# Order tables for all five engines, halved dense groups and paired layer norms in a two-layer attention and token-mixing kernel

## The chip, the cores and the metric

The kernel runs on one core of one Trainium2 chip. Its time is device microseconds of one execution; the time before is 478.1 us, the median of 6 runs from 476.24 to 480.12. A profile is one more execution that the hardware profiler recorded. Its engines are PE (TensorE's matmuls, with PEld for the weight loads), DVE (VectorE), ACT (ScalarE), POOL (GpSimd) and SP (SyncE, which issues the DMAs).

## What is computed

Two layers, the same weights in both, on x of 2048 tokens by 512 features in bf16. Each layer adds sliding-window attention and then a token-mixing MLP to x:

```python
def _A_ref(x, wqkv, wo):
    H = 32; Dh = D // H; W = 256
    q, k, v = ...                        # x @ wqkv, 32 heads of 16
    scores = einsum("bhqd,bhkd->bhqk", q, k) * (Dh ** -0.5)
    mask = (idx[:, None] - idx[None, :] >= 0) & (idx[:, None] - idx[None, :] < W)
    p = softmax(where(mask, scores, -1e9))
    return einsum("bhqk,bhkd->bhqd", p, v) ... @ wo
def _B_ref(x, w1, b1, w2, b2):
    h = _layernorm(x)
    u = gelu(einsum("bsd,sf->bdf", h, w1) + b1)      # mixes tokens: 2048 -> 1792
    return einsum("bdf,fs->bds", u, w2) + b2         # 1792 -> 2048, back to (s, d)
x = x + _A_ref(_layernorm(x)); x = x + _B_ref(_layernorm(x))     # twice
```

`_B_ref` is given a layer norm of x and takes another, so the kernel applies one formula for both (`twice` in `ln_block`).

## The kernel before

**Tiles and stages.** The 2048 tokens are 16 tiles of 128 partitions, grouped in four chunks of 512 tokens. For a chunk m the stages are:

- `prepare` (L1052): in layer 1 first the previous MLP's second product for its four tiles (`y_block`, L1032, 14 matmuls of 512 columns in entries of four, four, four and two); then the layer norm of the tiles (`ln_block`, L682: two statistics instructions on DVE, L686 and L688, two small ones on POOL, L691 and L693, and the scaling on DVE, L697), and `qkv` (L727).
- `qkv`: four transposes on PE into PSUM (L747), their copies to `xhT` (L731 on DVE or L733 on ACT), then K and Q of head group o (`proj`, four matmuls of 512 columns, L764) and V for four pairs of 64-token blocks (`vproj`, L794, in two entries of eight matmuls each). K is written as `kbd`, two masked copies. For chunk 0 of both layers ACT makes them straight from PSUM (L773, the set `KACT`), else a staging copy and two POOL instructions do (L780).
- `attention` (L826): for each of four head groups, four (chunk 0) or five pieces. A piece is one score entry on PE (L848, 8 or 12 matmuls into two pairs of PSUM banks), two exps on ACT of 1024 elements each (L860, some of 768), and masks on DVE (L873, L876). The pieces of a head group end in one P·V entry on PE (L894, 72 or 112 matmuls). Its result is copied by DVE (L938), its denominators travel over SP's queue: `rr` (L940), reciprocal on DVE (L947), `rscr` to DRAM (L949), `md` back, broadcast (L952), with four `cs` moves beside them (L944); POOL multiplies (L956). The last head group of the last chunk takes its denominators from matmuls instead (L907).
- `wo_block` (L962): the output projection (L966), added to x on DVE (L970), and the layer norm for the MLP.
- `u_part` (L998): the first product of the MLP for some chunks, 14 output tiles (L1012). Partial sums are held in `ub` (L1021, L1024); the last part ends in Gelu on ACT (L1027).

`STEPS` (L125) gives the order in which a layer's stages are recorded. In layer 0 parts u0, u1, u2 and U3 are separate, in layer 1 u0 and u1 are one.

**Scores are counted below** from 0 in layer 0 (0 to 75) and on in layer 1 (76 to 151).

**What sets the order.** Nothing is issued as it is recorded. `op` (L171) notes an operation with the engines that may run it, what it reads and writes, and a cost. `schedule` (L350) then runs a list scheduler: at each step `_pick` (L264) offers each engine's best candidate, scores first, P·V next, dense work by a priority that `fprio` (L708) makes from the place of recording plus a table of offsets, `RANK` (L21). `_place` (L215) gives PSUM banks and buffers, with a limit on the banks of each class (`small`, `big`, `sc`). `reorder` (L420) then moves entries by the offsets of a second table, `MOVES` (L35), and `emit` (L429) writes each engine's list with the semaphore waits it needs. `mm_group` (L714) cuts a dense product in entries of `STEP` = 4 matmuls, which is the grain at which other work can come between.

All loads go through SP, in the order of its list. At the start these are x tiles 0 to 3 one by one, then V's columns of wqkv (512 KB), x tiles 4 to 7 (512 KB), K's first block, x tiles 8 to 11, Q's first block (128 KB each), a bias, K's other blocks (384 KB), a bias, Q's other blocks, and later x tiles 12 to 15 and Wo. w1 comes in 28 loads of 256 KB a layer through four buffers (L981), w2 in 56 of 128 KB (L992).

## Time and profile before

| | |
|---|---|
| median of 6 runs | 478.1 us |
| profiled execution, its own time | 479.17 us |
| its span | 477.4 us |
| PE, DVE, ACT, POOL busy | 438.0, 365.9, 327.1, 126.7 us |
| exps (L860) | 304, 284.1 us busy |
| first exp starts, last exp of layer 0 ends | 16.45 us, about 174 us |
| L1012 and L1035, matmuls of 512 columns | 448 each, 108.3 and 103.7 us busy |
| chain that ended last | PE 64%, ACT 21%, DVE 7% |

A busy time is the union of an engine's instructions. PE's matmuls overlap in their pipeline, so the 380 ns of one are not its pace: forty-two matmuls of 512 columns in a row take 9.06 us, 0.216 each. "Idle before" with a releaser names what ended the wait.

### The profile page before, as it was taken

Reading aid. Unit: us, or ns where it says so; the run is one execution under the profiler, and the core shown is the slowest. Engines: PE = TensorE matmul, PEld = TensorE weight load, DVE = VectorE, ACT = ScalarE, POOL = GpSimd, SP = SyncE. Lnnn points to the kernel's source line nnn. Section 1 sums busy time; section 2 is a strip of 40 time slices with the busy share of each in tenths; the row PEclk is TensorE's granted clock in tenths of the full one; section 3 lists DMA queues with packets and bytes.
Section 4 is the critical chain, followed back from the end, with each engine's and each line's share of the span. In section 5 each row is a group of like instructions: output and inputs, shape, how many; then the busy total and the mean of one; then the engine's idle time right before and its main releaser. Section 6 shows DMA issues by size and latency. Waiting matters only on the chain.

```text
span 477.4 us, 15704 instructions
## 1 busy us (share of the span) xinstructions
PE 438.0 (92%) x6830; PEld 208.1 (44%) x6830; DVE 365.9 (77%) x746; ACT 327.1 (69%) x372; POOL 126.7 (27%) x197
## 2 busy tenths in 40 slices
PE   7889867889989789999989999999999999999997
PEld 4355433353333344455444453444543444444443
DVE  6998988879989979764687888989976786952222
ACT  1999998798989970545998799789888872061000
POOL 3222453271531213010012623352373131200000
PEclk9999999899999999999999999999999999999999
DMA  8513231222253424232054224251325545524654
GB/s 248 150 40 92 68 97 51 75 74 76 63 151 91 135 85 119 81 89 66 5 141 118 73 74 121 71 133 31 83 57 149 138 119 140 145 76 137 180 168 133
DMA packets 83993, 49.47 MB, mean 104 GB/s; under 512 B 14676, under 2 KB 78164, under 8 KB 83924
## 3 DMA queue, kind: packets, MB, share of 16 engines
q1 hardware_dynamic: 83924, 48.46, 36.5%
q8 instruction: 54, 0.88, 0.8%
q14 instruction: 15, 0.12, 0.1%
HBM read 41.43 MB, written 2.59 MB: 92 GB/s over the span
## 4 chain that ended last, share of the span: by engine, by line
PE 64%; ACT 21%; DVE 7%; DMA 2%; SPq 2%; issue 2%; POOL 1%; POOLq 0%
ACT pt L860 19%; PE PS L1012 18%; PE PS L1035 17%; PE PS L894 7%; PE PS L764 6%; PE PS L848 6%; PE PS L966 4%; PE PS L794 4%; DVE pt L876 1%; DMA w1b<-in_B_w_dram 1%; DVE cs L938 1%; PE PS L613 1%; ACT kbd L773 1%; SPq L992 1%; SPq L944 1%
## 5 line engine op out<-in xcount | busy, mean ns | idle before, releaser
L860 ACT ACTIVATE pt<-PS 128x1024 bf16<-128x1024 f32 (+1 forms) x304 | 284.1, 1027 | 33.1 <-PE PS L848 30.8
L1012 PE MATMUL PS<-xh_sb,w1b 128*128 128x512 bf16 x448 | 108.3, 384 | 2.4 <-DMA w1b<-in_B_w_dram 1.0
L1035 PE MATMUL PS<-ub,w2b 128*128 128x512 bf16 x448 | 103.7, 380 | 0.0
L848 PE MATMUL PS<-qT,kbd 32*128 32x64 bf16 (+4 forms) x1632 | 60.7, 244 | 20.3 <-ACT pt L860 11.0
L1012 PEld LDWEIGHTS PS<-xh_sb,w1b 128*128 128x128 bf16 x448 | 40.2, 98 | 56.3 <-issue 7.3
L956 POOL TENSOR_TENSOR oT<-cs,md 128x512 bf16<-128x512 f32 x30 | 39.3, 1309 | 93.3 <-DMA cs<-cs 51.2
L764 PE MATMUL PS<-xhT,wqkv 128*128 128x512 bf16 x256 | 62.5, 381 | 1.4 <-DVE vt L731 0.9
L1035 PEld LDWEIGHTS PS<-ub,w2b 128*128 128x128 bf16 x448 | 41.3, 98 | 50.1 <-issue 3.9
L1024 DVE TENSOR_TENSOR ub<-PS,ub 128x512 f32<-128x512 f32 x70 | 46.0, 684 | 17.6 <-PE PS L1012 17.3
L876 DVE TENSOR_TENSOR pt<-pt,ldm 128x1024 bf16<-128x1024 bf16 (+1 forms) x80 | 54.8, 699 | 3.2 <-ACT pt L860 3.1
L848 PEld LDWEIGHTS PS<-qT,kbd 32*128 32x128 bf16 x1632 | 23.3, 92 | 76.3 <-ACT pt L860 43.6
L780 POOL TENSOR_SCALAR kbd<-stg,par 128x512 bf16<-128x512 bf16 x48 | 38.1, 803 | 65.4 <-DVE stg L731 55.9
L938 DVE COPY cs<-PS 128x512 f32<-128x512 f32 x60 | 39.1, 684 | 16.3 <-PE PS L894 15.5
L1040 DVE SCALAR_TENSOR_TENSOR x_sb<-PS,bcol,x_sb 128x512 bf16<-128x512 f32 x32 | 23.3, 745 | 35.7 <-PE PS L1035 35.5
L1027 ACT ACTIVATE ub<-ub,bcol 128x512 bf16<-128x512 f32 x28 | 18.5, 713 | 45.9 <-DVE ub L1024 45.8
L894 PE MATMUL PS<-pt,vt 64*18 64x64 bf16 (+4 forms) x3040 | 40.4, 247 | 5.5 <-ACT pt L860 2.7
L873 DVE TENSOR_TENSOR pt<-pt,ldm 128x512 bf16<-128x512 bf16 (+1 forms) x104 | 40.2, 409 | 4.3 <-ACT pt L860 4.2
L686 DVE BATCH_NORM_STATS2 stats<-x_sb 128x6 f32<-128x512 bf16 x64 | 43.1, 682 | 0.5
L691 POOL TENSOR_SCALAR rstd<-agg 128x2 f32<-128x2 f32 (+1 forms) x40 | 9.4, 235 | 121.4 <-DVE agg L688 120.3
L894 PEld LDWEIGHTS PS<-pt,vt 64*18 64x18 bf16 x3040 | 31.5, 85 | 15.7 <-ACT pt L860 5.5
L764 PEld LDWEIGHTS PS<-xhT,wqkv 128*128 128x128 bf16 x256 | 21.9, 98 | 30.5 <-issue 4.3
L794 PE MATMUL PS<-wqkv,xhT 128*64 128x256 bf16 x512 | 33.6, 275 | 1.6 <-issue 0.6
(54 smaller groups left out, 327.0 us busy)
## 6 DMA issues: line engine op xcount, KB each, us to landing
w2b<-in_B_w_dram SPq DMA_DIRECT2D x112, 128.0 KB, 2.4
w1b<-in_B_w_dram SPq DMA_DIRECT2D x56, 256.0 KB, 3.4
md<-rscr SPq DMA_DIRECT2D x30, 256.0 KB
cs<-cs SPq DMA_DIRECT2D x120, 32.0 KB, 2.5
out_dram<-x_sb SPq DMA_DIRECT2D x16, 128.0 KB, 1.8
x_sb<-in_A_x_dram SPq DMA_DIRECT2D x3, 512.0 KB
wqkv<-in_A_wqkv_dram SPq DMA_DIRECT2D x2, 384.0 KB, 5.3
x_sb<-in_A_x_dram SPq DMA_DIRECT2D x4, 128.0 KB
```

The source lines that it names most:

```text
L686: op("vector", lambda e, t=t: e.bn_stats(stats[:, t, :], x_sb[:, t, :]), reads=[f"x{t}"], writes=[f"st{t}"], cost=dve_cost(512))
L764: mm_group(ft, 4, lambda e, c: e.matmul(PS[:, ft.slot, :], lhsT=wqkv[:, c, which * 512 + o * P:which * 512 + (o + 1) * P], rhs=xhT[:, tx.s ...
L794: last = e.matmul(PS[64 * hf:64 * hf + 64, ft.slot, sc * 256:(sc + 1) * 256], lhsT=xhT[:, tx.slot, c, tok:tok + 64], rhs=wqkv[:, c, 1024:1 ...
L848: last = e.matmul(PS[:, bank(r), c0 * 64:(c0 + nb) * 64], lhsT=kbd[32 * r:32 * r + 32, tkk.slot, jj, :, :].rearrange("p h n -> p (h n)"), ...
L860: return e.activation(pt[:, tp.slot, 2 * u:2 * u + 2, 0:n], PS[:, b0:b0 + 2, 0:n], ACTF.Exp, scale=SMSCALE)
L873: return e.tensor_tensor(v, v, msk.unsqueeze(1).to_broadcast([P, 4, w]), op=ALU.mult)
L876: return e.tensor_tensor(v, v, msk.unsqueeze(1).unsqueeze(1).to_broadcast([P, 4, k, w]), op=ALU.mult)
L894: last = e.matmul(PS[32 * r:32 * r + 18, tO[h].slot, q0 * 64:(q0 + nb) * 64], lhsT=vt[64 * h:64 * h + 64, tvv.slot, jj, 4 * o + r, :], rhs ...
L938: op("vector", lambda e, tO=tO[h], tc=tc, h=h: e.tensor_copy(cs[:, tc.slot, h], PS[:, tO.slot, :]), reads=[tO[h]], writes=[(tc, h)], cost= ...
L1012: out_ = e.matmul(PS[:, tu.slot, :], lhsT=w1b[:, tw.slot, s, tt * P:(tt + 1) * P], rhs=xh_sb[:, 4 * m + s, :], start=(n == 0 and s == 0), ...
L1024: op("vector", lambda e, tu=tu, ft=ft: e.tensor_tensor(uacc(ft), PS[:, tu.slot, :], uacc(ft), op=ALU.add), reads=[tu] + uk(ft), writes=uk( ...
L1035: mm_group(ft, NFT, lambda e, fc: e.matmul(PS[:, ft.slot, :], lhsT=w2b[:, tws[fc // W2F].slot, fc % W2F, k * P:(k + 1) * P], rhs=uT(fc), s ...
```

## The change

- **Order.** `schedule`, `_pick`, `RANK` and the class limits in `_place` go. `follow` takes one written list of recorded operations for each engine, `ORDER`, and walks all five, to give buffers and banks in the order of the same cost estimates. It makes no choice of order or engine. `MOVES` is applied after it, with new values.
- **Halved groups.** `STEP` is 2 in layer 0 and 4 in layer 1, for projections, Wo and the U parts but the last.
- **Layer norm in pairs.** Chunk 0's tiles are normalised two at a time too, as those of the other chunks: one L691 and one L693 for two tiles.
- **Loads.** Recorded order of the first loads: x tiles 0 to 3, K's first block, Q's first block, V's columns, the rest. In the built program SP issues them as `ORDER` and `MOVES` say: x tiles 0 to 3, V's columns, x tiles 4 to 7, K's first block, Q's first block, x tiles 8 to 11, K's others, Wo, x tiles 12 to 15, Q's others.
- **K's copies** in chunk 0 may run on DVE as well, one after the other. In the built program all 16 are on ACT, as before. One other copy of layer 0 goes from ACT to DVE.
- Some operations get tags, with no effect on the program.

The diff, tables and repeated parts cut:

```diff
 NTR, DTR = (4, 4), 600
 EVACT = {(0, 0), (0, 1), (1, 0), (1, 1)}
 XHP = set()
-RANK = (
...
+ORDER = (
...
 )
 MOVES = (
...
 )
 KACT = {(l, 0, o) for o in range(4) for l in range(2)}
@@ -215,17 +348,12 @@
     def _place(self, o):
 
 
-        t, got, taken, wcls = 0.0, [], {}, {}
+        t, got, taken = 0.0, [], {}
         for tl in o.tiles:
             if tl.slots is not None:
                 continue
             pool = tl.pool
             used = taken.setdefault(id(pool), set())
-            q = pool.classes.get(tl.cls)
-            if q:
-                c = wcls[tl.cls] = wcls.get(tl.cls, 0) + tl.n
-                if q[0] + c > q[1]:
-                    return None
             when = {s: max([x.done for x in ops], default=0.0) for s, ops in pool.free.items() if s not in used}
             if tl.n == 2:
...
-    def _pick(self, e, cand, ready, free, mode):
...
-    HOLD = 600.0
-    WINDOW = ({0: 400.0, 1: 250.0, 2: 50.0}, {0: 150.0, 1: 400.0, 2: 400.0})
+
     layer = 0
-    SLACK = {"scalar": 60.0, "tensor": 0.0}
 
     HAM = 3413.3
-    WARM = (216.0, 0.45)
     warm = None
 
     def _dummy(self):
@@ -347,48 +419,53 @@
             t += d
         return t - t0
 
-    def schedule(self):
+    def follow(self, orders):
+
         self.dummies = []
         self.busy, self.rates, self.ported = {}, [0.5], [0.0, 0.0]
         free = {e: 0.0 for e in self.ENGS}
-        cand = {e: [] for e in self.ENGS}
-        ready = {}
+        ready = {o.idx: 0.0 for o in self.ops}
         self.order = {e: [] for e in self.ENGS}
-        dma_free = 0.0
-        mode = None
-        for o in self.ops:
-            if o.ndeps == 0:
-                ready[o.idx] = 0.0
-                for e in o.engs:
-                    cand[e].append(o)
-        left = len(self.ops)
+        ptr = {e: 0 for e in self.ENGS}
+        lists = {}
+        for e, order in zip(self.ENGS, orders):
+            lists[e] = []
+            for i in order:
+                if i < 0:
+                    o = self._dummy()
+                    self.dummies.append(o)
+                    ready[o.idx] = 0.0
+                else:
+                    o = self.ops[i]
+                o.eng = e
+                lists[e].append(o)
+        dma_free, mode = 0.0, None
+        left = sum(map(len, lists.values()))
         while left:
             best = None
             for e in self.ENGS:
-                if cand[e]:
-                    got = self._pick(e, cand[e], ready, free[e], mode)
-                    if got and (best is None or got[0] < best[0]):
-                        best = (got[0], e, got[1])
+                if ptr[e] == len(lists[e]):
+                    continue
+                o = lists[e][ptr[e]]
+                if o.ndeps:
+                    continue
+                t = free[e] + (SWITCH if e == "tensor" and o.mode != mode else 0.0)
+                t = max(ready[o.idx], t)
+                if o.port:
+                    t = max(t, self.ported[e == "vector"])
+                if any(tl.slots is None for tl in o.tiles):
+                    at = self._place(o)
+                    if at is None:
+                        continue
+                    t = max(t, at[0])
+                if best is None or t < best[0]:
+                    best = (t, e, o)
             if best is None:
...
+                raise RuntimeError("orders are stuck")
             m, e, o = best
...
-            for x in o.engs:
-                cand[x].remove(o)
-            o.eng = e
+            ptr[e] += 1
+            left -= 1
             o.fn, o.cost = o.engs[e]
-            if o.idx < 0:
-                self.dummies.append(o)
             self._alloc(o)
             o.start = m
             if o.dma:
...
@@ -627,11 +699,9 @@
         def load_w(a, b):
             op("sync", lambda e: e.dma_start(wqkv[:, :, a * P:b * P], w_src[:, :, a * P:b * P]),
                writes=[f"w{i}" for i in range(a, b)], dma=True, cost=(b - a) * 420, lat=2300.0, prio=-1e6)
-        load_x(0, 1)
-        load_x(1, 2)
+        for t in range(4):
+            load_x(t, t + 1)
         load_w(4, 5)
-        load_x(2, 3)
-        load_x(3, 4)
         load_w(0, 1)
         load_w(8, 12)
         load_w(5, 8)
@@ -701,7 +771,7 @@
                     engs["gpsimd"] = (f, 760)
                 op(engs, None, reads=[f"x{t}", f"ag{t}", f"rs{t}"], writes=[f"xh{t}"], port=True)
 
-        STEP = 4
+        STEP = (2, 4)
 
         groups = [0]
 
@@ -709,12 +779,13 @@
 
             k = groups[0]
             groups[0] += 1
-            return 1e6 + len(g.ops) + (RANK[k] if k < len(RANK) else 0) + 1e-4 * k
+            return 1e6 + len(g.ops) + 1e-4 * k
 
         def mm_group(dst, n, mk, reads, cols=512, prio=None, holds=(), tag=""):
             prio = fprio() if prio is None else prio
-            for k0 in range(0, n, STEP):
-                k1 = min(n, k0 + STEP)
+            st = STEP[g.layer]
+            for k0 in range(0, n, st):
+                k1 = min(n, k0 + st)
 
                 def f(e, k0=k0, k1=k1):
                     last = None
@@ -769,11 +840,16 @@
                     op(*evac(lambda: qT[:, tq[o].slot, :], lambda: PS[:, ft.slot, :]), reads=[ft], writes=[tq[o]], prio=-1e4)
                     return
                 if kact:
+                    kp = []
                     for h in range(2):
-                        op("scalar", lambda e, h=h: e.activation(
-                            kbd[:, tk[o].slot, :, h, :], PS[:, ft.slot, :].rearrange("p (s n) -> p s n", n=64), ACTF.Copy,
-                            scale=par[:, h:h + 1]), reads=[ft, ("par", h)], writes=[(tk[o], h)], cost=act_cost(512, 1),
-                           prio=-1e4)
+                        src = lambda: PS[:, ft.slot, :].rearrange("p (s n) -> p s n", n=64)
+                        kp.append(op({
+                            "scalar": (lambda e, h=h: e.activation(kbd[:, tk[o].slot, :, h, :], src(), ACTF.Copy,
+                                                                   scale=par[:, h:h + 1]), act_cost(512, 1)),
+                            "vector": (lambda e, h=h: e.tensor_scalar(kbd[:, tk[o].slot, :, h, :], src(), par[:, h:h + 1],
+                                                                      0.0, op0=ALU.mult, op1=ALU.add),
+                                       dve_cost(512, psum=True, ptrs=1))},
+                            None, reads=[ft, ("par", h)], writes=[(tk[o], h)], prio=-1e4, after=kp[:1]))
                     return
                 op(*evac(lambda: stg[:, ts.slot, :], lambda: PS[:, ft.slot, :]), reads=[ft], writes=[ts], prio=-1e4)
                 for h in range(2):
@@ -1000,1 +1076,1 @@
-            cls, st = ("big", 1) if last else ("small", STEP)
+            cls, st = ("big", 1) if last else ("small", STEP[g.layer])
...
@@ -1053,9 +1129,7 @@
                 for t in range(4 * m, 4 * m + 4):
                     if layer:
                         y_block(t, w2t, cls)
-                    if m == 0:
-                        ln_block([t], False)
-                    elif t % 2:
+                    if t % 2:
                         ln_block([t - 1, t], False)
                 Q[m], K[m], V[m] = qkv(m, cls)
             for step in STEPS[layer].split():
@@ -1077,7 +1151,7 @@
             op("sync", lambda e, t=t: e.dma_start(out_v[:, t, :], x_sb[:, t, :]), reads=[f"x{t}"], dma=True, cost=500, lat=1000.0,
                prio=1e5)
 
-        g.schedule()
+        g.follow(ORDER)
         g.reorder(MOVES)
         block = es.enter_context(nc.Block())
         g.emit(block)
```

## The prediction

> **What bounds the kernel now.** I read the page's busy times first, then busy time by stretch, then the order of time of ACT and PE around each long idle time of ACT.
>
> ```profile
> PE 438.0 (92%) x6830; PEld 208.1 (44%) x6830; DVE 365.9 (77%) x746; ACT 327.1 (69%) x372; POOL 126.7 (27%) x197
> PEclk9999999899999999999999999999999999999999
> ...
> 16.40:174.50 158.10, 134.77 (x2862) 64.39 (x2860) 140.52 (x291) 145.17 (x162) 55.53 (x76) 0.98 0.30 83
> 174.50:223.50 49.00, 48.97 (x373) 23.61 (x374) 33.76 (x64) 17.87 (x27) 7.28 (x17) 1.00 0.34 99
> 223.50:391.70 168.20, 159.24 (x3011) 75.46 (x3007) 138.85 (x287) 146.06 (x161) 54.97 (x74) 1.00 0.34 92
> 391.70:474.00 82.30, 81.19 (x476) 37.04 (x474) 39.29 (x69) 12.68 (x18) 4.30 (x9) 1.00 0.49 140
> 85.20:88.60 3.40, 3.25 (x50) 1.29 (x39) 2.94 (x6) 1.76 (x2) 0.27 (x1) 0.50 0.51 159
> ```
>
> The stretches give us, then busy PE, PEld, DVE, ACT, POOL, then granted clock. Layer 0's attention (16.4 to 174.5) has ACT busy 92% of the time and PE 85%: ACT sets its pace. The dense stretches (174.5 to 223.5, and from 391.7) are PE alone, 99 to 100%. Layer 1's attention has PE at 95%, ACT at 87%. So a microsecond taken from ACT's idle time in layer 0's attention reaches the end, since after its last score PE runs without idle time into layer 1; elsewhere only a shorter PE helps.
>
> ACT's idle time between first and last exp of layer 0 is 158.1 - 145.2 = 13 us. The lines that carry it:
>
> ```profile
> 57.97 1.94 ACT L860 ACTIVATE pt<-PS 128x1024 bf16<-128x1024 f32 x2 [0.59 <-PE PS L848]
> 75.84 1.94 ACT L860 ACTIVATE pt<-PS 128x1024 bf16<-128x1024 f32 x2 [2.13 <-PE PS L848]
> 89.72 1.94 ACT L860 ACTIVATE pt<-PS 128x1024 bf16<-128x1024 f32 x2 [2.76 <-PE PS L848]
> 128.23 3.98 ACT L860 ACTIVATE pt<-PS 128x1024 bf16<-128x1024 f32 x4 [0.51 <-PE PS L848]
> 139.08 1.02 ACT L860 ACTIVATE pt<-PS 128x1024 bf16<-128x1024 f32 x1 [1.02 <-PE PS L848]
> ...
> 135.36 1.04 PE L1012 MATMUL PS<-xh_sb,w1b 128*128 128x512 bf16 x4 [0.43 <-ACT pt L860]
> 136.33 1.40 PE L894 MATMUL PS<-pt,vt 64*18 64x128 bf16 x112
> 137.66 1.04 PE L1012 MATMUL PS<-xh_sb,w1b 128*128 128x512 bf16 x4
> 138.62 0.40 PE L848 MATMUL PS<-qT,kbd 32*128 32x128 bf16 x12
> ```
>
> ACT waits for a score (L848) each time, and the score stands behind a lump on PE: a dense group of four, the 112 P·V matmuls, another dense group. A pair of exps takes 1.9 us, such a lump 3.0.
>
> **What the Trainium skill says.** "ScalarE: Activation LUTs", What ACT_TABLE_LOAD costs: an ACTIVATE takes 186 ns + 0.833 ns per element, and neighbours overlap by 93 ns. For 1024 elements 1,039 ns, one every 946; the trace has 1,038 and five in 4.78 us, so it agrees and an exp cannot be made shorter by order. "TensorE: Matmul & The Clock Gate", What's actually happening: half or full clock, decided by activity in free-running windows of about 3.4 us. The trace agrees: 0.50 in 85.2 to 88.6 and in 105.7 to 109.1, each behind a stretch with PE busy at most 1.9 of 3.4 us. "DMA: Bandwidth & Descriptors", Queues, rings and completion order: transfers that SyncE issues share one row of rings, taken in ring order; so a weight load moved behind others starts later. No run here isolates that.
>
> **The change part by part.** I compared the order of the built instructions with the order before.
>
> *Loads.* The source lists K's and Q's first blocks ahead of V's, but the order table does not: the program issues x tiles 0 to 3, V's 512 KB, x tiles 4 to 7, K's first block, Q's first block. Only Q's first block moves, ahead of x tiles 8 to 11. K's was issued at 3.66 us and lands some 5.2 later, 8.9. On PE, however, K and Q of head group 0 now stand behind three of V's eight half-groups, not behind all.
>
> *Start.* The last transposed tile is copied by 10.6 (ACT 9.99 + 0.58, DVE 10.21 + 0.42). Then K: four matmuls, 0.97, to 11.5 (before 12.50 to 13.5). Two K copies on ACT 1.27, to 12.8. Q follows K on PE to 12.4; its DVE copy stands behind three statistics of 0.65, so 12.8 + 0.69 = 13.5; score 0.4, first exp near 14.0 instead of 16.45. But ACT's work up to the fifth score's exp is the same set (8 K copies, 8 exps, 3 other copies): before from 12.61 to 26.04, of it 0.38 idle, so 13.05 us. After: 11.5 + 13.05 + 1.2 waiting for Q = 25.75. Gain 0.3 to 0.5, and one copy fewer on ACT in the layer (7 instead of 8, 0.6): **-1.0**. DVE takes that copy, 0.68, beside 12% idle time.
>
> *Halved groups.* In layer 0 projections, Wo and all U parts but the last go from four matmuls an entry to two: 90 more entries, the same matmuls. The totals before each fourth score are within 0.9 us of before; what changes is which side of a score a half falls. Behind P·V lumps, idle ACT time: score 20 0.59 loses a half V group 0.47; score 28 2.13 loses half a Wo group, 0.43; score 34 2.76 loses two U matmuls, at half clock 0.43 each (the warm-up, at half clock, has 12 in 4.88), 0.86 in all; score 53 0.51 loses its whole U group in front, all 0.51; score 58 1.02 loses two halves, 0.86; score 70 loses its 0.23. Sum 3.36. The halves go elsewhere: scores 48 and 59 now have 1.73 of dense work ahead of them, and an interval of that size shows 0.23 idle (132.45 and 149.25): +0.46. **-2.9**.
>
> *Mode changes.* PE changes between matmul layouts 342 times, before 331; ten of the eleven stand before the ninth score. One costs 0.11: a lone group of four takes 0.97, eight in a row 1.83. That is 1.1 us where PE idles 3.4 of 20 to 40 us; at nothing, and +1.1 if that cover is gone.
>
> *LN in pairs.* Eight POOL instructions fewer (0.2 and 0.56 us), hidden, POOL being busy 27%. A tile waits for its partner: in layer 1's first chunk the transpose of tile 1 stands 3.3 us of PE work behind tile 0's last y matmul, and the chain between them took about 3.4 (213.55 to 216.79 and its hops). **+0.2**, bounds 0 and 0.5; behind it on PE stand three more transposes and V.
>
> *SyncE's order.* Q's other three blocks are now issued behind Wo and x tiles 12 to 15, 1.05 MB more; at the first slice's 248 GB/s that is 4.2 us, landing near 17.7 instead of 13.46. Their first reader on PE comes near 18, and ACT has exps until 21. Nothing; at worst +2. Late in layer 1, loads 15 and 16 of w1 stand behind md's last load, which waits for a round trip through DRAM:
>
> ```profile
> 395.42 0.65 SPq L952 DMA_DIRECT2D md<-rscr  x1
> ...
> 399.54 3.61 PE L1012 MATMUL PS<-xh_sb,w1b 128*128 128x512 bf16 x16 [1.04 <-DMA w1b<-in_B_w_dram]
> ```
>
> Load 16 was issued at 394.20 and 15 at 393.02; they would go out near 395.6 and 396.6, with one 256 KB load less ahead of 16. The same PE instruction waits for it; dense work follows with no cover. **+0.3**, bounds -0.5 and +2.
>
> *Other order.* Layer 1's attention keeps its intervals but for swaps of one place: 0, bounds -1 and +1.
>
> Sum: -1.0 - 2.9 + 0.2 + 0.3 = -3.4. The profiled execution took 479.17 (span 477.4 and 1.8 around it), 1.1 above the median of 478.1. From the median, **474.7**; from the profiled one, 475.8. A difference of 0.5%, 2.4 us, is about what a measurement of this kernel can tell from no change.
>
> **Rivals.** *The clock takes it back.* If the steadier order does not lift PE out of half clock and two more windows fall to it, each costs half of 3.4 us: +3.4, so 478. For it: idle PE time in 81.8 to 85.2 comes from intervals that don't change; against: mean clock 0.98 leaves only two such windows. The same mechanism the other way, both windows gone, gives 471.3.
>
> *Mode changes cost more than 0.11.* Eleven changes in the stage where ACT is starved of scores: a lone score takes 0.40, and idle times of 0.16 to 0.45 stand before several. At 0.31 each (3.4 / 11) they eat the gain, from 0.53 ((3.4 + 2.4) / 11) the kernel is slower than can be mistaken; at 0.6, 478.1 - 3.4 + 6.6 = 481.3. For it: PE is nearly full from 8 to 20 us; against: 3.4 us idle after that.
>
> *SyncE becomes late.* PE waits 2 us for w1's loads instead of 0.3 and 2 us for Q's blocks: 474.7 + 1.7 + 2 = 478.4. For it: the lines above, 5.2 us from issue to landing; against: w1's 28 loads at 256 KB take 3.4 in the median, and three dense groups stand ahead of the reader of load 15.
>
> **How the numbers follow.** Sum as worked out 0.58 (its own range 472.5 to 477), both slow windows gone 0.08, two more slow windows 0.16, dear mode changes 0.10, late SyncE 0.08. Below 475.7: four fifths of the first and all of the second, 0.54. Above 480.5: the dear mode changes and tails of two others, 0.17. The rest, 0.29, is within. The range, 470.8 to 481, leaves out the tails.
>
> **What would show it.** First exp near 14 us; ACT's idle time before scores 28, 34 and 58 down to about 1.7, 1.9 and 0.2, and its sum in layer 0's attention from 13 to 9 or 10; last exp of layer 0 some 3.5 us earlier, near 170; the two dense stretches as long as before. Wrong if PE's idle time in the first 40 us grows, if PE waits for wqkv near 18 us, if a wait on w1b over 2 us shows in layer 1's last U part, or if more than two windows show half clock.

## The result and the profile after

The changed kernel takes 481.8 us in the median of the executions taken with the prediction (474.97 to 485.67, 35 of them), the kernel before 478.8 beside it (72). Ratio 1.0014, 95% interval 0.9996 to 1.0032: no difference that the measurement can tell from none, where 474.7, 0.7% faster, was forecast, and the median lies just above the range of 470.8 to 481. A median here counts every execution, a ratio leaves out those more than 1.5% above the fastest of their kernel (15 of the changed kernel's 35 here, 11 of 22 in r5 below, at most three in any other), which is why the two can differ by some tenths of a per cent. By medians the changed kernel is 0.6% slower here, and 0.3 and 0.2% in r1 and r9 below.

The profiled execution took 478.96 us (span 477.2, before 477.4). First its page, the busy line and the clock, then busy time by stretch with the columns as before (us; PE, PEld, DVE, ACT, POOL; clock; DMA), the stretches set at the changed kernel's own ends of stages:

```profile
PE 436.4 (91%) x6830; PEld 206.6 (43%) x6830; DVE 369.1 (77%) x747; ACT 326.7 (68%) x371; POOL 123.8 (26%) x189
PEclk9999999899999999999999999999999999999999
```

```profile
13.66:173.50 159.84, 138.69 (x2900) 65.56 (x2899) 140.73 (x299) 146.56 (x164) 54.20 (x76) 0.99 0.32 87
173.50:221.70 48.20, 47.67 (x370) 23.18 (x370) 33.09 (x64) 18.02 (x27) 6.32 (x13) 1.00 0.33 95
221.70:390.80 169.10, 157.38 (x3004) 75.47 (x2999) 145.41 (x289) 146.18 (x160) 54.27 (x73) 1.00 0.34 90
390.80:474.60 83.80, 82.39 (x480) 37.07 (x478) 39.67 (x67) 12.70 (x18) 5.36 (x11) 1.00 0.50 143
86.70:90.10 3.40, 3.40 (x20) 0.91 (x18) 1.98 (x3) 1.94 (x2) 0.00 (x0) 0.50 0.28 67
```

Two things are to be seen. Layer 0's attention starts earlier (13.66 against 16.45) and ends earlier, and one stretch at half clock is left of two. But in layer 1's attention, third line, PE is busy 157.4 of 169.1 us, 93%, where it had been 159.2 of 168.2, 95%: PE, which sets that stage's pace, now stands idle 11.7 us instead of 9.0. And DVE is busy longer, 145.4 us against 138.9 there, with two instructions more (289 against 287).

ACT's order of time where the forecast had named its idle times (columns: start, busy time in us, engine and line, operation, count, and in brackets the idle time before it with its releaser; the bracketed waits at 73.24, 87.73, 90.67, 135.53 and 137.98 are those ahead of scores 28, 34, 35, 58 and 59):

```profile
73.24 3.77 ACT L936 ACTIVATE pt<-PS 128x1024 bf16<-128x1024 f32 x4 [0.51 <-PE PS L924]
...
87.73 1.94 ACT L936 ACTIVATE pt<-PS 128x1024 bf16<-128x1024 f32 x2 [3.38 <-PE PS L924]
90.67 2.85 ACT L936 ACTIVATE pt<-PS 128x1024 bf16<-128x1024 f32 x3 [1.00 <-PE PS L924]
...
135.53 1.94 ACT L936 ACTIVATE pt<-PS 128x1024 bf16<-128x1024 f32 x2 [0.61 <-PE PS L924]
137.98 1.94 ACT L936 ACTIVATE pt<-PS 128x1024 bf16<-128x1024 f32 x2 [0.51 <-PE PS L924]
```

Score 28's wait fell from 2.13 to 0.51, score 58's from 1.02 to 0.61, but score 34's grew from 2.76 to 3.38, ahead of and into the half-clock stretch, and score 35 behind it has a new one of 1.00. What of this is due to the order is taken up below.

Where the time went is told best by the start of each score's first exp, changed kernel minus kernel before, in us, from the two traces. The first row is this profile; the next two are two more profiles of the same kernel (r1 and r9 below). The last is r3 below, which has layer 0 in the order of the kernel before, layer 1 in that of the changed kernel, and ran at full clock in both layers' attention.

| profile | score 0 | 12 | 44 | 75 (last of layer 0) | 76 (layer 1) | 116 | 151 (last) |
|---|---|---|---|---|---|---|---|
| changed | -2.79 | -0.97 | -3.03 | -2.29 | -1.84 | -2.84 | -0.88 |
| changed, r1 | -3.00 | -1.18 | -3.68 | +0.04 | +0.09 | -0.58 | +3.06 |
| changed, r9 | -3.32 | -1.49 | -6.06 | -1.38 | -0.93 | -2.10 | +0.12 |
| r3 | -0.49 | -0.36 | -3.10 | -1.91 | -1.04 | -2.13 | -0.31 |

The profile of the kernel before had two stretches at half clock in layer 0, so it is a slow measure there: r3, with the same layer 0 order, is 1.9 us ahead of it at score 75. Against r3 the changed kernel is 0.4 us ahead at score 75 in its first profile, 2.0 behind in r1 (each with a stretch at half clock near 85 us), and in r9, at full clock, 3.0 ahead at score 44 and 0.5 behind at score 75. One profile against another is good to a microsecond or two at best, as the three of one kernel show. But the pattern is plain: what start and layer 0 gain is given back, late in layer 0 in r1 and r9, and in the second half of layer 1's attention (score 116 is near 310 us of 222 to 391) in all four rows, 1.8 to 3.6 us between score 116 and the last. The 3.6 are r1's, which had a second stretch at half clock there, from 354.0 to 357.4 us.

Here is one of the places in layer 1, from the order of time of the changed kernel, VectorE, GpSimd and TensorE around 348 us:

```profile
346.92 0.41 DVE L949 TENSOR_TENSOR pt<-pt,ldm 128x512 bf16<-128x512 bf16 x1
347.25 1.67 DVE L767 TENSOR_SCALAR xh_sb<-x_sb,agg,rstd 128x512 bf16<-128x512 bf16 x1
348.85 1.28 DVE L802 CAST stg<-PS 128x512 bf16<-128x512 f32 x2
...
346.31 1.24 POOL L763 TENSOR_TENSOR rstd<-rstd,mhalf 128x2 f32<-128x2 f32 x1
347.51 1.26 POOL L1032 TENSOR_TENSOR oT<-cs,md 128x512 bf16<-128x512 f32 x1
...
347.99 0.40 PE L924 MATMUL PS<-qT,kbd 32*128 32x64 bf16 x12
350.18 0.40 PE L924 MATMUL PS<-qT,kbd 32*128 32x128 bf16 x12 [1.79 <-DVE stg L802]
```

One xh_sb, which takes 0.41 us elsewhere, takes 1.67: it begins beside the rstd power on GpSimd and does not end before oT, which follows at once, has ended at 348.77. Behind it in VectorE's order stand the two copies into stg, and behind those PE waits 1.79 us with a score. In the kernel before the same two copies follow a mask, with no GpSimd instruction that holds them up:

```profile
348.74 0.41 DVE L873 TENSOR_TENSOR pt<-pt,ldm 128x512 bf16<-128x512 bf16 x1
349.07 1.28 DVE L731 CAST stg<-PS 128x512 bf16<-128x512 f32 x2
...
350.41 0.40 PE L848 MATMUL PS<-qT,kbd 32*128 32x128 bf16 x12 [0.53 <-DVE stg L731]
```

The Trainium skill has the mechanism: "SBUF — State Buffer", Who interferes with whom, says that VectorE and GpSimd share one pair of SBUF ports, that it is an exclusive lock, that whoever issues first has it for the whole instruction while the other is blocked, and that a VectorE instruction takes it when it has two inputs in SBUF (against a GpSimd instruction that reads SBUF) or when it is a tensor_scalar in a two-port mode. The masks are the first kind; xh_sb, a tensor_scalar with one tensor input, can only be the second. This trace agrees (0.41 us against 1.67), and so it does on the other side: a copy into qT from PSUM at 345.70 to 346.39 ran beside a kbd product at 345.65 to 346.34 and took its usual 0.69.

### The profile page after: what moved, and what is told of

Its sections match the earlier page's. It is cut to its first block, busy times and chain, and to the rows that moved or that the text cites. A ratio compares the mean times of both kernels' runs of the same rounds, so it can differ in the third digit from the quotient of the medians.

```text
span 477.2 us, 15700 instructions
## 1 busy us (share of the span) xinstructions
PE 436.4 (91%) x6830; PEld 206.6 (43%) x6830; DVE 369.1 (77%) x747; ACT 326.7 (68%) x371; POOL 123.8 (26%) x189
## 4 chain that ended last, share of the span: by engine, by line
PE 59%; ACT 19%; DVE 12%; DMA 4%; POOL 2%; SPq 1%; issue 1%; POOLq 0%
ACT pt L936 19%; PE PS L1111 18%; PE PS L1088 15%; PE PS L835 7%; PE PS L924 6%; PE PS L970 5%; PE PS L1042 4%; PE PS L870 3%; DVE cs L1014 2%; DVE xh_sb L767 2%; DMA x_sb<-in_A_x_dram 1%; DVE pt L949 1%; DVE stats L756 1%; DMA w1b<-in_B_w_dram 1%; DVE pt L952 1%
## 5 line engine op out<-in xcount | busy, mean ns | idle before, releaser
L835 PE MATMUL PS<-xhT,wqkv 128*128 128x512 bf16 x256 | 63.7, 381 | 0.0
L952 DVE TENSOR_TENSOR pt<-pt,ldm 128x1024 bf16<-128x1024 bf16 (+1 forms) x80 | 52.9, 677 | 1.6 <-ACT pt L936 0.9
L761 POOL TENSOR_SCALAR rstd<-agg 128x2 f32<-128x2 f32 (+1 forms) x36 | 8.4, 235 | 147.4 <-DVE agg L758 146.7
L949 DVE TENSOR_TENSOR pt<-pt,ldm 128x512 bf16<-128x512 bf16 (+1 forms) x104 | 42.2, 423 | 3.5 <-ACT pt L936 3.1
L970 PE MATMUL PS<-pt,vt 64*18 64x64 bf16 (+4 forms) x3040 | 39.3, 242 | 3.4 <-ACT pt L936 1.5
L870 PE MATMUL PS<-wqkv,xhT 128*64 128x256 bf16 x512 | 34.8, 276 | 2.7 <-issue 1.1
L1042 PE MATMUL PS<-wo_sb,oT 128*128 128x512 bf16 x128 | 32.9, 380 | 0.9 <-POOL oT L1032 0.8
```

The lines of the kernel that those rows point to most:

```text
L835: mm_group(ft, 4, lambda e, c: e.matmul(PS[:, ft.slot, :], lhsT=wqkv[:, c, which * 512 + o * P:which * 512 + (o + 1) * P], rhs=xhT[:, tx.s ...
L870: last = e.matmul(PS[64 * hf:64 * hf + 64, ft.slot, sc * 256:(sc + 1) * 256], lhsT=xhT[:, tx.slot, c, tok:tok + 64], rhs=wqkv[:, c, 1024:1 ...
L949: return e.tensor_tensor(v, v, msk.unsqueeze(1).to_broadcast([P, 4, w]), op=ALU.mult)
L952: return e.tensor_tensor(v, v, msk.unsqueeze(1).unsqueeze(1).to_broadcast([P, 4, k, w]), op=ALU.mult)
L970: last = e.matmul(PS[32 * r:32 * r + 18, tO[h].slot, q0 * 64:(q0 + nb) * 64], lhsT=vt[64 * h:64 * h + 64, tvv.slot, jj, 4 * o + r, :], rhs ...
L1042: mm_group(ft, 4, lambda e, o, i=i, ft=ft: e.matmul(PS[:, ft.slot, :], lhsT=oT[:, tos[o][0].slot, i * P:(i + 1) * P], rhs=wo_sb[:, o, :], ...
```

## The experiments

Theory A: the changed kernel's new VectorE and GpSimd orders bring more such meetings, and these take back what start and halved groups gain. Theory B: the clock and the chance of one execution decide, not the orders. The table gives the median of each kernel, that of the kernel before measured beside it on the same chip, their ratio and its 95% interval.

| run | kernel | median us (n) | before us | ratio | interval |
|---|---|---|---|---|---|
| r1 | changed | 480.72 (22) | 479.31 | 1.0025 | 1.0005 to 1.0046 |
| r2 | changed to 180 us, then before | 475.66 (6) | 479.31 | 0.9909 | 0.9874 to 0.9943 |
| r3 | before to 180 us, then changed | 479.72 (14) | 479.31 | 1.0018 | 0.9995 to 1.0042 |
| r4 | changed to 295 us, then before | 473.89 (6) | 479.31 | 0.9883 | 0.9842 to 0.9923 |
| r5 | changed, 4 GpSimd held | 478.78 (22) | 480.12 | 0.9923 | 0.9896 to 0.9951 |
| r6 | changed, 4 VectorE moves | 479.91 (22) | 480.12 | 0.9998 | 0.9973 to 1.0023 |
| r7 | start only | 484.47 (6) | 480.12 | 1.0098 | 1.0061 to 1.0135 |
| r8 | halved groups only | 477.24 (22) | 480.12 | 0.9944 | 0.9921 to 0.9968 |
| r9 | changed | 480.41 (22) | 479.30 | 1.0015 | 0.9994 to 1.0035 |
| r10 | as r5 | 477.17 (20) | 479.30 | 0.9940 | 0.9914 to 0.9966 |
| r11 | as r4 | 474.89 (9) | 479.30 | 0.9918 | 0.9885 to 0.9951 |
| r12 | as r4, 10 GpSimd held | 472.58 (6) | 479.30 | 0.9860 | 0.9829 to 0.9891 |
| r13 | changed, 14 GpSimd held | 475.41 (8) | 479.95 | 0.9906 | 0.9872 to 0.9941 |
| r14 | before, 6 GpSimd held | 479.26 (14) | 479.95 | 0.9979 | 0.9949 to 1.0009 |
| r15 | start only, mended | 480.76 (14) | 479.95 | 1.0020 | 0.9993 to 1.0047 |

**Which part of the program loses (r1 to r4).** A mixture takes the work that starts before a given time (in the trace of the kernel before) in one kernel's order on each engine, and the rest in the other's. Nothing is left out. For that the program gets the final order of every engine, and for every pool which tile has which buffer in turn, as tables:

```diff
-        g.follow(ORDER)
-        g.reorder(MOVES)
+        g.follow(ORDER, SLOTS)
```

With layer 0 from the kernel before (r3) its groups are whole, with layer 1 from it (r2) its layer norms are single.

> The changed kernel once more, on the chip that also runs the three mixtures, to see whether the late stalls of its first profile recur. Theory A (the new VectorE and GpSimd orders give back in layer 1's attention what layer 0 gained): 478 to 480 us, at most 1 us from the kernel before; the profile again leads by 2 to 3.5 us at the last score of layer 0 and at score 114, and again loses 2.5 us or more between score 114 and the end, with TensorE waits of 1 us or more near 321 and 350 us. Theory B (the losses of that profile are chance of one execution, and the clock or the spread decides): the gaps near 321 and 350 us are elsewhere or gone.

> All work that starts in the first 180 us in the changed kernel's orders (its halved groups, its start, its pairs of layer norms), all later work in the order of the kernel before. Theory A: the lead of 1.8 to 2.3 us that the changed kernel's profile has at the end of layer 0 stays to the end, 476.0 to 477.5 us. Theory B (layer 0's lead is lost anyway, through the clock or in the wait for the weights of the output blocks): 478 to 479.5 us, no better than the changed kernel.

> The other half: the kernel before up to 180 us, the changed kernel's orders from there. Theory A: no lead at score 76; from there to the end the changed kernel lost 1.6 to 1.9 us against its own lead, so 480 to 481.5 us, slower than before by 1 to 2.5 us. Theory B: like before, 478 to 479.5 us, with no new TensorE waits near 320 and 350 us.

> The changed kernel's orders up to 295 us (start, layer 0, the dense stretch and the first third of layer 1's attention), the kernel before from there. Theory A: the changed kernel led by 3.0 to 3.8 us at score 114, and nothing after it is new, so 475.0 to 476.5 us. Theory B: 477.5 us or more.

r2 and r4 kept the lead, 0.9 and 1.2% (r11, the repeat of r4, 0.8%), both by more than was expected of them. r3, the other half, gained nothing; the 480 to 481.5 us expected came out at 479.7, within its interval of no loss, though its profile loses 1.8 us between score 116 and the last as the theory says. r1 met the late waits but not the lead of 2 to 3.5 us at layer 0's last score: it had none. The waits are in the orders: in the profiles of the changed kernel, of r1 and of r3 PE waits at the same scores for the same VectorE instructions, and in before and r4 these waits are smaller or absent.

| PE's wait, us | before | changed | r1 | r3 | r4 | r5 (4 held) | r6 (moved) |
|---|---|---|---|---|---|---|---|
| score 118 for qT, near 313 us | 0.45 | 1.12 | 1.12 | 1.12 | 0.46 | 0.45 | 0.45 |
| transposes of xh_sb, near 321 | 0 | 1.21 | 1.08 | 1.08 | 0 | 0 | 0.39 |
| score 134 for stg, near 350 | 0.53 | 1.79 | 1.79 | 1.75 | 0.53 | 0.53 | 0.45 |

So these waits are not the chance of one execution: they are the same in three, one of which (r3) ran at full clock throughout the attention of both layers, and absent in r4. The clock, the other half of theory B, is on record for every execution, not for the profiled ones alone. This table takes them together; the last two columns are the executions whose mean granted clock was 0.998 or more.

| kernel | executions | mean clock | of these at 0.998 or more | their mean us |
|---|---|---|---|---|
| before (beside r1 and r9) | 79 | 0.998 | 50 | 479.0 |
| changed (first, r1, r9) | 79 | 0.994 | 14 | 478.9 |
| changed to 295 us, then before (r4, r11) | 15 | 0.999 | 14 | 475.2 |
| changed, 4 GpSimd held (r5, r10) | 42 | 0.995 | 14 | 475.4 |
| changed, 14 GpSimd held (r13) | 8 | 0.997 | 4 | 474.4 |

The changed kernel was granted 0.994 each of the three times, and the less an execution was granted the longer it took (correlation of clock and time -0.70 to -0.77). A stretch of 3.4 us at half clock lowers the mean of 477 us by 0.0036, so by this estimate an execution had about one such stretch more than one of the kernel before. The changed kernel's median over all 79 is 481.3, 2.4 us above the mean of those at full clock. But these, at 478.9, have no gain over the kernel before either, where r4, r11 and the kernels with GpSimd held (below) have 3.6 to 4.6. So what comes with the lower clock accounts for the changed kernel's median above the kernel before, and for part of its distance from r2 and r4, which ran at 0.9997 in the mean; it does not account for the missing gain. Why the changed kernel is granted less was not found, nor whether the clock falls first or follows a delay.

**Is it the neighbour or the order (r5, r6, r10).** r5 leaves all orders alone and makes four GpSimd instructions of layer 1 wait for the VectorE instruction that they had met; r6 leaves GpSimd alone and moves the stretched instruction behind what PE waits for.

```diff
         g.reorder(MOVES)
+        at = {o.idx: o for o in g.ops}
+        for pool, dve in ((1705, 1953), (1608, 1787), (1969, 1872), (2188, 2081)):
+            at[pool].extra.append(at[dve])
```

```diff
         g.reorder(MOVES)
+        dve = g.order["vector"]
+        at = {o.idx: o for o in dve}
+        for late, than in ((1953, 1617), (1786, 1792), (1787, 1786), (1872, 1847), (2081, 1929)):
+            dve.remove(at[late])
+            dve.insert(dve.index(at[than]) + 1, at[late])
+        for i, o in enumerate(dve):
+            o.seq = i
```

> The changed kernel with every order unchanged, but four GpSimd instructions of layer 1 (the oT products with numbers 5, 8 and 13 and one kbd half) made to wait until the VectorE instruction beside them is done (mask 55, xh_sb of token blocks 17, 20 and 25), so that the two no longer run side by side. Theory A1 (the VectorE instructions that TensorE waits for are stretched by the GpSimd instruction beside them): mask 55 falls from 1.48 us to 0.42, the xh_sb from 1.35, 1.67 and 1.30 us to 0.41; TensorE's waits near 313, 321, 350 and 390 us (1.12, 1.21, 1.80 and 0.88 us) shrink by 3 to 4 us together, and about 0.8 of it is lost again in the wait for a w1 block at the end: 476 to 478 us, 1 to 3 us under the kernel before. Theory A2 (the order of the VectorE queue alone is at fault, the neighbour on GpSimd is not): durations and waits as in the changed kernel, 479 to 481 us, or more, since oT comes later.

> The changed kernel with four moves on VectorE alone, in layer 1: mask 55 behind the copy into qT that TensorE waits for, xh_sb of blocks 16 and 17 behind the x_sb sum of block 14, xh_sb 20 behind two copies into stg, xh_sb 25 behind a copy into ub. GpSimd's order is unchanged. Theories A1 and A2 both: what TensorE waits for near 313, 321, 350 and 390 us is now ahead of the stretched instruction, 3 to 4 us of waits gone, 476 to 478 us. Theory C (the losses of layer 1 have another cause, such as the new order of the DMAs on SyncE): the waits come back behind other instructions, 479 to 481 us.

> The changed kernel with four GpSimd instructions of layer 1 held until the VectorE instruction beside them is done, once more, since its first time was spread from 472 to 486 us. Theory A1 (what layer 1 loses is VectorE stretched beside GpSimd): 2 to 3.5 us under the changed kernel of the same call, and 0.4 to 0.8 per cent under the kernel before; from score 116 to the last score within 0.6 us of the kernel before's pace, where the changed kernel lost 2.0 and 3.6 us in its two profiles. Theory B (the time is decided by the granted clock and by chance, not by those waits): the median within 1 us of the changed kernel's.

A wait added made the kernel faster. r5 showed it in its profile, but its median of 478.8 missed the 476 to 478 us expected, with executions from 472 to 486; hence r10. There the same place as above, in order of time:

```profile
341.22 0.40 DVE L767 TENSOR_SCALAR xh_sb<-x_sb,agg,rstd 128x512 bf16<-128x512 bf16 x1
341.54 1.28 DVE L802 CAST stg<-PS 128x512 bf16<-128x512 f32 x2
...
340.27 1.39 POOL L763 TENSOR_TENSOR rstd<-rstd,mhalf 128x2 f32<-128x2 f32 x1
341.70 1.27 POOL L1032 TENSOR_TENSOR oT<-cs,md 128x512 bf16<-128x512 f32 x1
...
342.87 0.40 PE L924 MATMUL PS<-qT,kbd 32*128 32x128 bf16 x12 [0.53 <-DVE stg L802]
```

oT starts a moment later, 0.04 us after rstd, xh_sb takes 0.40 instead of 1.67 and loses nothing beside rstd, and PE waits 0.53 instead of 1.79. In r5 mask 55 fell from 1.48 us to 0.40, and the three xh_sb from 1.35, 1.67 and 1.30 to 0.41, 0.40 and 0.41. From score 116 to the last, r5 and r10 gained 0.4 and 0.6 us on the kernel before, where the changed kernel had lost 2.0 to 3.6; both profiles are of faster executions than their medians (475.1 and 472.8 us). Ratio 0.994 in r10, against 1.0015 for the changed kernel measured with it: 0.75%, 3.6 us, by the medians 3.2. A1 stands, and A2, for which nothing should have changed, falls.

r6 is the miss: 479.9 us, where A1 and A2 said 476 to 478 and theory C, another cause such as SyncE's order, 479 to 481. The three waits in the table went as expected (its last column), but xh_sb of token block 25 still took 1.21 us beside an oT, and a mask of 0.68 took 2.41 near 353 us and one of 0.41 took 2.26 near 357. The second of these in VectorE's, GpSimd's and PE's order of time:

```profile
356.56 2.26 DVE L949 TENSOR_TENSOR pt<-pt,ldm 128x512 bf16<-128x512 bf16 x1
358.75 0.68 DVE L952 TENSOR_TENSOR pt<-pt,ldm 128x1024 bf16<-128x1024 bf16 x1
359.35 0.41 DVE L949 TENSOR_TENSOR pt<-pt,ldm 128x512 bf16<-128x512 bf16 x1
359.68 1.27 DVE L1097 COPY ub<-PS 128x512 f32<-128x512 f32 x2
...
356.62 0.69 POOL L856 TENSOR_SCALAR kbd<-stg,par 128x512 bf16<-128x512 bf16 x1
357.28 1.26 POOL L1032 TENSOR_TENSOR oT<-cs,md 128x512 bf16<-128x512 f32 x1
...
360.51 1.36 PE L970 MATMUL PS<-pt,vt 64*18 64x128 bf16 x112 [1.22 <-DVE ub L1097]
```

The mask lasts as long as the kbd product and the oT together, the copies into ub behind it are late, and PE waits 1.22 at the P·V entry behind them. The meetings passed on to other instructions, and the time stayed, 0.9998. That the waits come back elsewhere is as theory C had it; its cause is not needed, since what comes back is again VectorE beside GpSimd, and r10 gained with SyncE's order as it was. Moving one partner of a meeting was not enough here.

**The parts by themselves (r7, r8, r15).** The start alone is the mixture cut at 45 us. Halved groups alone have the order of the kernel before to 45 us and from 180 us on, with single layer norms everywhere.

> Only the start: the work that begins in the first 45 us in the changed kernel's orders, the rest as before. The prediction's step Start says 1.0 us faster: 477.5 to 478.7 us, with the first exponential near 13.7 us and a lead of 0.8 to 1.0 us from score 8 on that stays to the end. Rival: the lead is lost at the next transfer that is late, 479 to 479.6 us.

> Only the halved groups with their orders, from 45 to 180 us; the start and everything from 180 us on as before. The prediction's step Halved groups says 2.9 us faster: 476.0 to 477.0 us. Rival (mode changes or the new VectorE and GpSimd orders of layer 0 take it back): 478.5 to 479.5 us.

> Only the start again, with the fault of its first mixture mended: on SyncE, the four w2 loads that each wait for the one before go behind the rr copies that stood behind them. If the step Start is right: 1.0 us faster than before, 477.8 to 478.8 us, a lead of 0.8 to 1.5 us at score 8 that stays. Rival (the start's lead does not outlive the first chunk): 479 to 480 us.

r8 measured 0.56% (0.32 to 0.79), 2.7 us of 480; the step said 2.9. Its mean clock, 0.998, was that of the kernel before (0.997). r7 lost 1% by a fault of its own at the seam. SyncE's queue, VectorE's and ACT's order of time in r7:

```profile
46.12 7.30 SPq L1183 DMA_DIRECT2D w2b<-in_B_w_dram  x5
53.46 0.51 SPq L1135 DMA_DIRECT2D cs<-cs  x1
55.56 0.37 SPq L1183 DMA_DIRECT2D w2b<-in_B_w_dram  x1
55.97 1.48 SPq L1135 DMA_DIRECT2D cs<-cs  x1
57.50 0.60 SPq L1131 DMA_DIRECT2D rr<-cs  x1
...
59.51 0.35 DVE L1138 RECIPROCAL rr<-rr 128x32 f32<-128x32 f32 x1 [5.65 <-DMA rr<-cs]
...
62.61 1.94 ACT L1051 ACTIVATE pt<-PS 128x1024 bf16<-128x1024 f32 x2 [5.32 <-PE PS L1039]
```

Each w2 load waits for an earlier one to land, the copy of rr stands behind them in the queue, and VectorE's reciprocal, PE's next score and ACT stand behind that: 5.3 us of ACT. r15 puts four w2 loads (1197, 1200, 1203 and 1206 in SyncE's list) behind the copy of rr (272):

```diff
-        659, 243, 241, 1194, 1197, 1200, 1199, 1203, 212, 1206, 209, 272, 244, 246, 276, 278, 242, 247, 1198, 274, 304,
-        275, 279, 305, 1202, 310, 307, 273, 311, 306, 308,
+        659, 243, 241, 1194, 1199, 212, 209, 272, 244, 246, 1197, 276, 278, 242, 247, 1200, 1198, 274, 304, 275, 279,
+        1203, 305, 1202, 310, 1206, 307, 273, 311, 306, 308,
```

It still gained nothing, 1.002: its lead was 0.8 us at score 13 and gone at score 14, where PE waits 0.89 for a copy into xhT, at the seam again. What the start is worth without the halved groups is therefore open: its lead of 1.0 to 1.5 at score 12 is in all profiles of the changed kernel, and r2 (start and halves) stands 0.35% below r8 (halves), with intervals that overlap.

**All of it (r9, r11 to r14).** r9's profile had shown two more meetings, in layer 0, near 132 and 137 us; in that profile the clock was full there. VectorE, GpSimd, PE and ACT in r9:

```profile
136.37 2.35 DVE L952 TENSOR_TENSOR pt<-pt,ldm 128x1024 bf16<-128x1024 bf16 x2
138.64 0.68 DVE L1100 TENSOR_TENSOR ub<-PS,ub 128x512 f32<-128x512 f32 x1
...
136.50 1.66 POOL L1032 TENSOR_TENSOR oT<-cs,md 128x512 bf16<-128x512 f32 x1 [3.60 <-DMA md<-rscr]
...
139.37 1.47 PE L1088 MATMUL PS<-xh_sb,w1b 128*128 128x512 bf16 x6 [1.33 <-DVE ub L1100]
...
141.23 1.94 ACT L936 ACTIVATE pt<-PS 128x1024 bf16<-128x1024 f32 x2 [0.90 <-PE PS L924]
```

oT starts when md lands. Two masks of 0.68 take 2.35 beside it, the sum into ub comes late, PE waits 1.33, ACT 0.90. r1 had the same two meetings, the first profile had not: if it is md's landing that varies between executions, as these three suggest, so does what layer 0 loses. r12, r13 and r14 hold ten, fourteen and six instructions in the manner of r5, in the mixture of r4, in the changed kernel and in the kernel before:

```diff
-        for pool, dve in ((1705, 1953), (1608, 1787), (1969, 1872), (2188, 2081)):
+        for pool, dve in ((1705, 1953), (1608, 1787), (1969, 1872), (2188, 2081), (540, 778), (774, 951), (806, 644),
+                          (838, 959), (1011, 1063), (1437, 1511), (1501, 1550), (1769, 1985), (2065, 2168), (2156, 2236)):
```

> The changed kernel beside the next three kernels on one chip, as their measure. As before: 0 to 0.5 per cent slower than the kernel before, 479 to 481 us.

> The mixture that was fastest so far (the changed kernel's orders up to 295 us, the kernel before from there), with more runs than the six it had. Theory A1: 474 to 476 us, 0.9 to 1.2 per cent under the kernel before. Theory B: the first six were lucky, 477 to 479 us.

> The same mixture with ten GpSimd instructions (the oT products) held until the VectorE instruction beside them is done: those ten that its profile shows started up to 0.45 us before a mask or an xh_sb which then took 0.6 to 1.1 us more than its usual time. Theory A1: the ten take their usual 0.41 and 0.68 us; TensorE's waits of 1.31 us near 141 and 0.71 us near 361 us go, 1 to 2 us in all: 472 to 474.5 us. Rival: those waits are hidden or oT comes too late for the output product that reads it: no change against the mixture, 474 to 476 us, or 1 us more.

> The changed kernel, its orders untouched, with fourteen GpSimd instructions held instead of four: the four of layer 1 and ten more that three profiles of it showed beside a stretched mask or xh_sb (the oT products 7, 8, 9, 10, 13 of layer 0 and 0, 2, 7, 11, 12 of layer 1). Theory A1 in full (all that keeps the changed kernel from its forecast is this meeting of VectorE and GpSimd): 473 to 475.5 us, with its runs within 5 us of each other, level with the mixture to 295 us or under it. Theory A3 (the four of layer 1 were the whole of it, and the 2 us between that kernel and the mixture come from layer 1's other order): 476.5 to 478 us.

> The kernel before with its own six meetings taken away in the same manner (oT 0, 5 and 11 and one kbd half of layer 0, oT 2 and 7 of layer 1 wait for the mask beside them). Theory A1: the kernel before pays for such meetings too, but for fewer, so 477 to 478.7 us, 0.5 to 2 us faster. Rival (in the kernel before they fall where nothing waits for VectorE): 479 to 479.8 us, no change.

r13 took 475.4 us, 0.9906 of the kernel before, with its eight executions between 473.4 and 477.1: the forecast's 474.7 for the changed kernel (0.993), with every order untouched. Groups by line of VectorE (busy us, mean ns of one; idle time before) show the difference; first before:

```profile
L873 DVE TENSOR_TENSOR pt<-pt,ldm 128x512 bf16<-128x512 bf16 x72 | 32.6, 465 | 2.3 <-ACT pt L860 2.2
L697 DVE TENSOR_SCALAR xh_sb<-x_sb,agg,rstd 128x512 bf16<-128x512 bf16 x64 | 25.7, 426 | 2.8 <-POOL rstd L693 2.4
```

the changed kernel:

```profile
L949 DVE TENSOR_TENSOR pt<-pt,ldm 128x512 bf16<-128x512 bf16 x72 | 34.1, 483 | 0.9 <-ACT pt L936 0.8
L767 DVE TENSOR_SCALAR xh_sb<-x_sb,agg,rstd 128x512 bf16<-128x512 bf16 x64 | 29.9, 492 | 1.5 <-POOL rstd L763 1.1
```

and r13:

```profile
L949 DVE TENSOR_TENSOR pt<-pt,ldm 128x512 bf16<-128x512 bf16 x72 | 29.6, 420 | 1.6 <-ACT pt L936 1.4
L767 DVE TENSOR_SCALAR xh_sb<-x_sb,agg,rstd 128x512 bf16<-128x512 bf16 x64 | 26.3, 435 | 1.5 <-POOL rstd L763 1.1
```

The sum of the two rows rose from 58.3 to 64.0 us with the change and is 55.9 when the meetings are held apart. Counted over all of VectorE, instructions over 0.25 us longer than the median of their line and shape were 12 in the kernel before (7.9 us in excess), 16, 20 and 21 in the three profiles of the changed kernel (11.6, 15.0, 15.2), 7 in r13 (3.3) and 8 in r12 (3.0). r6 had 16 (12.0), and r4 17 (12.7) in its profile, which at 478.7 us was its slowest execution. Against r3's layer 0, in the order before and at full clock, r10 and r13 lead by 3.5 us at layer 0's last score, which is the forecast's figure.

r14 gained 0.2%, with an interval that holds zero: the kernel before has meetings too, but its rival expectation, no change, is as near as the theory's. Its profile shows that a hold has a price as well: an oT held until 267.51 us puts the kbd products behind it late for score 98, PE waits 1.32 us for them, where it had waited 0.31 in the kernel before, and the profile falls back by 1.4 us there. Whether that price or the lack of anything that waits for the meetings kept r14 from gaining was not settled. The mixture with ten held, r12, is the fastest of all, 472.6 us, 1.4% below the kernel before, its six executions within 1.2 us; it ran at a mean clock of 0.999. Between r10 and r13 the intervals overlap, so how much of the rest the ten further holds bring was not settled.

## Why the prediction was wrong, point by point

*Other order* is the step that failed: "Layer 1's attention keeps its intervals but for swaps of one place: 0, bounds -1 and +1." That was read from TensorE's order alone. VectorE's and GpSimd's orders were not compared as a pair, though the kernel's masks, xh_sb and oT all read and write SBUF, and for those of layer 0 the sum had no term at all. The diff above holds the hint: `if o.port` keeps such operations of the two engines apart in the program's own cost estimates, while nothing in the built program does. The value of the step, by the changed kernel against the same with the meetings held, is 1.0015 against 0.9906, some 5 us (r9 and r13, on two chips; 4.4 at full clock), of which 3.2 to 3.6 in layer 1 (r9 against r10, on one); 0 and the bound of +1 were the mistake.

*Halved groups*, -2.9: right in size (r8, 2.7 us, 1.5 to 3.8), not in its places, so in part by luck. Its waits were read from one profile, with half clock at score 34. In r3, r7, r14 and r15, with whole groups there and full clock, score 34 waits 1.63 to 2.10 instead of 2.76, as it does with halved groups where the clock is full (1.6 in r13, 1.9 in r9). So its fall to about 1.9, 0.86 of the sum's 3.36, comes without the halving. In the first profile it was 3.38, behind a pause of PE told below and at half clock. Score 28 waits 1.0 to 1.1 in r3, r7 and r14 (2.48 in r15) and 0.51 with halved groups in all but r4 and r12 (1.47, 2.01), so about 0.5 us is the halving's, near the 0.43 forecast. Scores 58 and 59 kept 0.6 and 0.5.

*Start*, -1.0: first exp at 13.1 to 13.7 us instead of 14.0, a lead of 1.0 to 1.5 at score 12. As a part of the whole it fits; by itself it could not be shown.

*Mode changes*, 0: r13 has every mode change of the changed kernel and reaches the forecast, so the rival "mode changes cost more" falls.

*LN in pairs*, +0.2: not isolated. From score 75 to score 76 the lead shrank by 0.2 to 0.6 us in r9, r10 and r13 (pairs) and by 0.3 in r2 (single in layer 1), so no price of pairs is seen there beyond a few tenths.

*SyncE's order*: Q's late blocks made nothing wait near 18 us. The wait for w1 near 399 us was forecast to grow by 0.3; it fell from 1.04 to 0.23. This is the line of the changed kernel's order of time:

```profile
400.56 1.02 PE L1088 MATMUL PS<-xh_sb,w1b 128*128 128x512 bf16 x4 [0.23 <-DMA w1b<-in_B_w_dram]
```

The U group that waits stands about 1 us later than the one that waited in the kernel before (400.56 against 399.54), which is room for the load. The rival "SyncE becomes late" falls too.

*The clock takes it back*: in part, but not the main cause. The changed kernel's first profile had one stretch at half clock where before had two, and r9 had none in its whole attention and still took 479.7. Over all executions the changed kernel was granted less, 0.994 against 0.998, and its median lies some 2 us above its executions at full clock; these, at 478.9, are inside the range, with the gain as absent.

Of what the prediction had asked for as evidence, r13 has most: first exp at 13.3 us, ACT's idle time in layer 0's attention down from 12.5 to 9.2 (forecast 9 to 10), its last exp near 169 us, no stretch at half clock in the attention. It does not have the waits of the single scores (0.51, 1.62 and 0.59 before 28, 34 and 58). In the changed kernel that idle time was 11.6, 14.2 and 13.0.

## What to carry to other kernels

When a change rewrites the orders of VectorE and GpSimd, compare the two lists side by side in time, not each by itself: a VectorE instruction with two SBUF inputs or in a two-port mode that starts beside a GpSimd instruction can have to wait that one out, and the next one too, as here 0.4 us became up to 2.3, and what stands behind it on VectorE waits as well. A kernel whose GpSimd work has slack can hold it with a semaphore until the VectorE instruction is through; here fourteen such waits were worth some 5 us in the changed kernel, and six in the kernel before nothing that could be told from zero. And a single profile with a stretch at half clock is a poor base for a sum of tenths: compare with one at full clock, and look at the clock of all executions. An order that only keeps the bounding engine's intervals says nothing of the engines that feed it.

## What the runs showed of the hardware that had not been expected

A meeting cost a short VectorE instruction between 0.4 and 1.9 us: masks of 0.42 us took up to 1.5 beside an oT of 1.27, xh_sb of 0.41 took 0.79 beside a kbd product of 0.69, the mask of r6 2.26 beside two instructions, and of several GpSimd instructions in a row it sometimes waited for one, not for all (xh_sb at 39.93 to 40.72, kbd products at 39.79 to 40.58 and 40.56 to 41.27 in the changed kernel). At 347.25 it waited for two, though it began 0.26 before the second, and the mask of r6 likewise. GpSimd was stretched too: in r10 the rstd power took 1.39 us beside two masks at 340.26 to 341.30, against 0.70 at 38.41 in the changed kernel. Which of two waiting instructions is served next was not settled.

TensorE paused ahead of the first U group of layer 0, near 85 us, with nothing to wait for that the trace shows. In the changed kernel's order of time:

```profile
82.77 0.33 PE L970 MATMUL PS<-pt,vt 64*18 64x256 bf16 x8
85.50 1.63 PE L1088 MATMUL PS<-xh_sb,w1b 128*128 128x512 bf16 x6 [2.40 <-DVE cs L1014]
```

The group reads xh_sb, complete at 83.43, and w1, whose first load was issued at 39.16; cs, which the line names, is no source of it, and in r13, with the same orders, the group starts at 83.83, before cs is complete at 84.31. Of the 2.4 us, 2.1 have no owner. The same pause was 0.06 us in the kernel before, at most 0.8 in r3, r7, r14 and r15, 0.9 to 1.2 in most others, 2.0 in r1 and 2.7 in r6. Among the kernels with halved groups, half clock began during or just after it in the three profiles with 2 us or more (at 86.7, 84.4 and 84.5 us) and in none with less than 1.3; but the kernel before had half clock at 85.2 with a pause of 0.06, so a link is not shown. What makes the pause was not found.
